# A weight conversion with a scaled exponent, its integer addition on VectorE, and a late reader of a GpSimd maximum

## Chip, cores and metric

One core of one Trainium2 chip runs the whole program. The metric is the device time of one execution in microseconds; the median of 3 runs of the kernel before is 634.65 us (633.98 to 636.14).

## The reference, cut to what matters

Three layers run one after the other on float data (4 batches, 8 heads, 768 steps, head size 48; so 3072 tokens of width 384). The weights of the middle layer (384 x 2048 and 2048 x 384) come in as 64-bit floats.

```python
for t in range(S):                                  # layer 1: linear attention with decay
    cur = einsum('bhd,bhe->bhde', u[None] * kt, vt)
    y[:, :, t] = einsum('bhd,bhde->bhe', rt, state + cur)
    state = wt[..., None] * state + einsum('bhd,bhe->bhde', kt, vt)
h = x @ w_in                                        # layer 2: x is y, 3072 x 384
x = (h * sigmoid(1.702 * h)) @ w_out
logits = x @ phi                                    # layer 3: soft mixture, 8 experts, 32 slots
d = softmax over tokens(logits); slot_input = d.T @ x
slot_out[e] = relu(slot_input[e] @ w1[e]) @ w2[e]
out = softmax over slots(logits) @ slot_out
```

## The kernel before

**Work and stages.** The 3072 tokens are cut into 6 blocks u of 512 (128 steps of each of 4 batches). A block needs 4 attention units (one a batch b; 24 in all, built by unit_nodes), then its share of layer 2 (mm_nodes): for each of 16 slices f of the hidden width, 9 matmuls h (L746), the GELU on ScalarE twice (L750 rounded, L754 full), the remainder on VectorE (L758), 9 matmuls x (L766 to L768). Each 32-bit operand is split into a high and a low part, so 3 matmuls stand for one product. Block 1 is done in two halves of 256 columns. After each block, moe2_nodes updates the running softmax over tokens: transposes, logits (L833), row maxima, exponentials, sums (L892). At the end come the experts (L1100, L1142) and the output (L1182 to L1198).

**Weight conversion.** conv_nodes(f) turns the weights of slice f from 64-bit floats into high and low parts: load raw (L477), ScalarE reads the upper words' magnitude (L482) and scales the lower words down (L483), VectorE clamps (L486), shifts the bits by 3 and masks (L490) and merges the sign (L494), GpSimd or VectorE adds the lower words' bits (L498), ScalarE writes the high part (L501), VectorE the low part (L504). There are two raw buffers and three of the tile cq. In the profiled execution all 16 additions ran on GpSimd.

**Order.** No loop sets the order: every step is a node with a cost, its predecessors, a priority (lower comes first) and buffers taken, and a list scheduler (Plan) simulates the engines and writes each engine's instructions in the order that it finds. Each engine's queue then runs in that order on the chip. Loads are all issued by SyncE (SP), in one queue. Conversion f has priority CONV0 + CONVD * f, attention unit b of block 0 ATT0 + ATTD * b and up to 9 more for its last step, units of block 1 start at 76, layer 2 of block 0 at 42. Loads whose names stand in SOON come first. Steps of VectorE marked port=True and steps of GpSimd exclude each other in the plan, in this form:

```python
if (e == "POOL" or e == "DVE" and s[7]) and port > now + 1e-9:      # L123, in Plan.order
    continue
...
if e == "POOL" or e == "DVE" and s[7]:
    port = free[e]                                                  # L139
```

The GELU remainder (L773) is so marked; the row maximum, softmax and copy steps of moe2_nodes are not.

**The range check.** lim (L570) sums decay factors into chk; inside0 compares them when all units are done, inside1 takes the maximum over partitions on GpSimd (L1023), inside2 reads it on VectorE (L1027), and inside3 loads it into a register at the very end, where a general kernel would run instead if a value were out of range. GpSimd takes two other such maxima: an early one over zeros (L953) and that of the softmax at the end (L1039). At the last attention unit's end GpSimd also has fills and copies (consts3, si0).

Of the kernel before, what the change touches and what calls it, by code (L numbers as in the profile page):

```python
# [8 lines left out]
F32 = mybir.dt.float32  # L9
# [3 lines left out]
AF = mybir.ActivationFunctionType  # L13
ALU = mybir.AluOpType
AX = mybir.AxisListType
PSUM = bass.MemoryType.PSUM

P = 128
NB, NH, NS, DH = 4, 8, 768, 48
DM = NH * DH  # L20
FF = 2048
NF = FF // P
# [7 lines left out]
EPS = 1e-9  # L30
W_TINY, W_HUGE = 2.0 ** -15, 122879.9921875
F_MOST = 2.0 ** 40
RAWB, CQB, NEW = 2, 3, 8

WIDE = (T, T // 2, T, T, T, T)

KTU = (2, 3, 4, 5)
C2E = {"DVE": 1.16, "POOL": 1.95}
RUKE = ({"DVE": 1.12}, {"POOL": 2.1})
QVE = ({"DVE": 0.56}, {"POOL": 1.05})  # L40
PIECES = (192, 192)
# [2 lines left out]
SOON = "w0 r0 c0 n0 u w1 r1 v0 n1 v1 w2 r2 n2 v2 c1 w3 r3 n3 v3"  # L44

FIRST, SECOND, PERIOD, LAG, AHEAD = 42.0, 150.0, 82.0, 4.2, 74.0
CONV0, CONVD, CONVL = 0.0, 6.0, 16.0
ATT0, ATTD = 3.0, 6.0
LAT = {"PE": 0.3, "ACT": 0.25, "DVE": 0.2, "POOL": 0.2, "DMA": 2.2, "X": 0.0}
SAME = {"PE": 0.0, "ACT": 0.2, "DVE": 0.12, "POOL": 0.1, "DMA": 2.2, "X": 0.0}  # L50
FROM = {"PE": 1.9, "ACT": 2.0, "DVE": 1.0, "POOL": 1.0, "DMA": 0.9}
# [3 lines left out]
def act(n):  # L55
    return 0.17 + n / 1200


def dve(n, rate=960):
    return 0.16 + n / rate  # L60
# [294 lines left out]
def rwkv_moe_softmoe_kernel(tc: tile.TileContext, ark, aw, nat, vr, ub, wf, phi, w1, w2, r, k, v, w, ug, out):  # L355
    nc = tc.nc
    pe, ve, ac, gp, sy = nc.tensor, nc.vector, nc.scalar, nc.gpsimd, nc.sync
# [16 lines left out]
    N = plan.add  # L374
    t_ = {}
# [12 lines left out]
    tick = cst.tile([P, 1], F32, name="tick")  # L388
    mfin = cst.tile([P, 1], F32, name="mfin")
    sm = {n: cst.tile([P, NSL], F32, name=n) for n in ("big", "mx", "rz")}  # L390
    chk = sm["rz"][0:ROWS, 0:NU * NB]
    ubt = ap1.tile([P, DM], F32, name="ubt")
    ind = ap1.tile([ROWS, NH, CH], F32, name="ind")
# [3 lines left out]
    m2 = {}  # L397
# [11 lines left out]
    def begin(blk):  # L409
        return FIRST if blk == 0 else SECOND + PERIOD * (blk - 1)  # L410
# [43 lines left out]
    def soon(key, pr):  # L454
        keys = SOON.split()
        return keys.index(key) - 100.0 if key in keys else pr
# [11 lines left out]
    def conv_nodes(f):  # L468
        pr = CONV0 + CONVD * f
        raw, cq, wk = f"raw{f}", f"cq{f}", f"w{f}"  # L470

        def words(t):
            return t_[raw].rearrange("p q n t -> p (q n) t")[:, :, t]

        def load():
            t_[raw] = cp1.tile([P, 2, DM, 2], I32, tag="raw", name=raw, bufs=RAWB)
            sy.dma_start(t_[raw].rearrange("p q n t -> p q (n t)"), wf[2 * f:2 * f + 2].rearrange("q p n -> p q n").bitcast(I32))  # L477

        def c0():
            wt[f] = wp.tile([P, 2, 2 * DM], F32R, tag="w", name=f"w{f}")  # L480
            t_[cq] = cp1.tile([P, 2 * DM], F32, tag="cq", name=cq, bufs=CQB)
            ac.activation(t_[cq], words(1).bitcast(F32), AF.Abs)  # L482
            ac.activation(words(0), words(0).bitcast(U32), AF.Copy, scale=2.0 ** -29)  # L483

        def c1a():
            ve.tensor_scalar(t_[cq], t_[cq], W_TINY, W_HUGE, op0=ALU.max, op1=ALU.min)  # L486

        def c1b():
            a = t_[cq].bitcast(I32)
            ve.tensor_scalar(a, a, 3, 0x3FFFFFF8, op0=ALU.logical_shift_left, op1=ALU.bitwise_and)  # L490

        def c1c():
            a = t_[cq].bitcast(I32)
            ve.scalar_tensor_tensor(a, words(1), -0x40000000, a, op0=ALU.bitwise_and, op1=ALU.bitwise_or)  # L494

        def c2(e):
            a = t_[cq].bitcast(I32)
            onto[e].tensor_tensor(a, a, words(0), op=ALU.add)  # L498

        def c3():  # L500
            ac.activation(wt[f][:, 0], t_[cq], AF.Copy)  # L501

        def c4():
            ve.tensor_tensor(wt[f][:, 1], t_[cq], wt[f][:, 0].bitcast(F32), op=ALU.subtract)  # L504

        n = N("DMA", 2.2, load, pr=soon(f"c{f}", pr - CONVL), take=[("raw", raw)])
        n = N("ACT", 2 * act(2 * DM), c0, [n], pr, take=[("cq", cq), ("w", wk)], use=[raw])
        n = N("DVE", dve(2 * DM, 1920), c1a, [n], pr, use=[cq], port=True)
        n = N("DVE", dve(2 * DM, 1920), c1b, [n], pr, use=[cq], port=True)
        n = N("DVE", dve(2 * DM), c1c, [n], pr, use=[raw, cq], port=True)  # L510
        n = N(C2E, 0, c2, [n], pr, use=[raw, cq], port=True)
        n = N("ACT", act(2 * DM), c3, [n], pr, use=[cq, wk])
        conv[f] = N("DVE", dve(2 * DM), c4, [n], pr, use=[cq, wk], port=True)


    limits, grp_last = [], {}
# [401 lines left out]
    for f in range(NF):  # L918
        conv_nodes(f)
# [23 lines left out]
    tend = begin(NU)  # L943
# [6 lines left out]
    nep = N("X", 0.0, open_ep, att_all, 0)  # L950
# [63 lines left out]


    def inside0():
        t_["cm"] = m2["ep"].tile([P, 2], F32, name="cm")
        ve.memset(t_["cm"], -1.0)
        ve.tensor_scalar(chk, chk, F_MOST, -1.0, op0=ALU.is_le, op1=ALU.mult)
        ve.tensor_reduce(t_["cm"][0:ROWS, 0:1], chk, axis=AX.X, op=ALU.max)  # L1020

    def inside1():
        gp.partition_all_reduce(t_["cm"][:, 1:2], t_["cm"][:, 0:1], P, reduce_op=bass_isa.ReduceOp.max)  # L1023
# [5 lines left out]
    def inside3():  # L1029
        t_["rv"] = nc.values_load(t_["out"][0:1, 0:1], min_val=0, max_val=1, skip_runtime_bounds_check_because="one less a comparison's 0 or 1")  # L1030

    n = nin = N("DVE", 0.35, inside0, limits + [nep], tend - 70)
    n = N("POOL", 0.57, inside1, [n], tend - 29)
    nok = N("DVE", 0.1, inside2, [n], tend - 28)

    G = grp_last
    n = N("DVE", 0.07, f0, [G["mx"]], tend - 59)
    n = N("DVE", 0.16, f1, [n, ncon], tend - 59)
    n = N("POOL", 0.57, lambda: gp.partition_all_reduce(sm["mx"], sm["big"], P, reduce_op=bass_isa.ReduceOp.max), [n], tend - 59)  # L1039
    n = N("DVE", 0.15, f3, [n], tend - 59)  # L1040
    n = N("ACT", 0.12, f4, [n, G["ex"]], tend - 59)
    n = N("DVE", 0.1, lambda: ve.tensor_tensor(sm["mx"], sm["mx"], sel, op=ALU.mult), [n], tend - 59)
# [3 lines left out]
    nsi = N("POOL", 0.68, si0, [nep], tend - 40, take=[("xl", "scrB")])  # L1046
    nsi = nsi0 = N("DVE", 0.17, f7, [n6, nz, nsi], tend - 59, use=["sp", "scrB"])

    finish[0](nsi)


    ctn, cpn = {}, {}
    for u in range(NU):
# [26 lines left out]
        n = N("DVE", 0.66, cs, [cnn[u], nep, cpn.get(u - 2), cpn.get(u - 1)], p0, take=[("xt", "scrA")] if u == 0 else [], use=["scrA"])  # L1080
        n = cpn[u] = N("PE", 0.44, cp, [n], p0, take=[("ps", kp)] + ([] if fin5 else [("a", kp)]), use=["scrA"])
# [7 lines left out]
    for g in range(2):  # L1089
        for hf in range(2):  # L1090
# [27 lines left out]
            n = N("PE", 2.8, e1, [nsi] + [ew[k] for k in keys], p0, take=[("ps", kh)], use=keys + ["scrB"])  # L1118
            own = [ks] if place else ["scrB"]
            n = N("ACT", 0.5, er, [n], p0, take=[(place[0], ks)] if place else [], use=[kh] + own)  # L1120
            n = N("PE", 0.44, et, [n], p0 - 1, take=[("ps", kt)], use=own)
# [4 lines left out]
    c0 = 0  # L1126
    for i, wd in enumerate(PIECES):
# [5 lines left out]
        for g in range(2):  # L1133
# [3 lines left out]
            def e2(p, g=g, ko=ko, wd=wd, at0=at0):  # L1137
                b = t_[ko] if p else bank(ko)
                for n in range(8 * p, 8 * p + 8):
                    a, k, j = at0[n], n // 4, n % 4  # L1140
                    w = t_[f"w2_{a // (4 * DM)}"][:, a % (4 * DM):a % (4 * DM) + wd]
                    pe.matmul(b[32 * j:32 * j + 32, :wd], hv[g]()[:, k, 32 * j:32 * j + 32], w, start=(k == 0), stop=(k == 7))  # L1142
# [8 lines left out]
            n = None  # L1151
            for p in range(4):
                keys = list(dict.fromkeys(f"w2_{a // (4 * DM)}" for a in at0[8 * p:8 * p + 8]))
                at = p0 + 0.5 + p if i and g else p0 - 1 + g + 0.1 * p
                n = N("PE", 0.17 + 0.425 * w_, lambda p=p, e2=e2: e2(p), [n] + hTn[g, p // 2] + [ew[k] for k in keys], at, take=[("ps", ko)] if p == 0 else [], use=keys + [ko])
# [14 lines left out]
        n = N("PE", 0.43 * w_, comp, ns + [ncon3], p0 - 3, take=[("ps", kz)], use=[f"sb{g}{i}" for g in range(2)])  # L1170
        n = N("ACT", 0.06 + 0.1 * w_, skh, [n], p0, take=[("gh", kk)], use=[kz])
        nsk = N("DVE", 0.07 + 0.13 * w_, skl, [n], p0, use=[kk, kz])
        per = min(NB, 512 // wd)
        for u in range(NU):
            kot, oe = f"ot{i}_{u}", []
            for q in range(NB // per):
# [16 lines left out]
                n = N("PE", 0.38 if wd <= P else 0.22, fin, [nsk, ctn[u]], p0 + 3 + u, take=[("ps", kf)], use=[kk])  # L1193
                n = N({"DVE": 0.07 + 0.53 * per * wd / 512, "ACT": 0.06 + 0.42 * per * wd / 512}, 0, oev, [n] + oe, p0, take=[("w", kot)] if q == 0 else [], use=[kf, kot])
# [79 lines left out]
```

## Time and profile before

| what | value |
|---|---|
| median of 3 runs | 634.65 us (633.98 to 636.14) |
| time of the profiled execution | 633.73 us |
| its span, first to last instruction | 631.9 us |
| TensorE busy | 570.4 us (90%) |
| VectorE busy | 431.6 us (68%) |
| ScalarE busy | 274.9 us (44%) |
| GpSimd busy | 90.3 us (14%) |
| mean granted TensorE clock | 0.99 |

PE is TensorE, PEld its weight loads, DVE VectorE, ACT ScalarE, POOL GpSimd, SP SyncE, which issues the loads. Durations come from the one profiled execution; what lies around its span is 1.8 us. A clock of 1.00 is the upper of TensorE's two levels (2.4 GHz), 0.50 the lower (1.2 GHz). Busy TensorE time is modelled and can hold overlaps, so stretches of it are compared by counts of instructions too.

### The profile page before, as it was taken

How to read it: one execution, taken by the hardware profiler on the slowest of the kernel's cores; microseconds unless marked ns; L12 is line 12 of the kernel's file. 1: busy time of each engine (PE TensorE's matmuls, PEld its weight loads, DVE VectorE, ACT ScalarE, POOL GpSimd, SP SyncE). 2: the span in 40 equal slices, each digit the busy share in tenths (PEclk: the TensorE clock that was granted, in tenths of full speed). 3: DMA queues.
4: the chain of work that ended last, by engine and by line, in shares of the span. 5: the costliest groups of instructions: out<-in, count | busy, mean ns of one | idle time of the engine just before them, and what ended most of it. 6: DMA issues, size and time to landing. Idle time of an engine off the chain costs nothing.

```text
span 631.9 us, 12380 instructions
## 1 busy us (share of the span) xinstructions
PE 570.4 (90%) x5092; PEld 462.7 (73%) x5092; DVE 431.6 (68%) x830; ACT 274.9 (44%) x524; POOL 90.3 (14%) x83
## 2 busy tenths in 40 slices
PE   3446899979999999999999999999999969999992
PEld 2445688767889999778877787877788757887362
DVE  9999797899999998787669766787672323112301
ACT  5544566573834443543316432444242333324232
POOL 3121232221111111111012202111120000000000
PEclk9999999999999999999999999999999989999997
DMA  8776434632343333032223232330210294467747
GB/s 294 233 240 209 140 104 158 215 150 76 115 114 114 107 108 113 7 107 74 91 76 101 55 110 77 101 113 28 74 39 1 95 357 147 153 229 249 306 152 219
DMA packets 29475, 86.08 MB, mean 136 GB/s; under 512 B 3040, under 2 KB 12384, under 8 KB 29408
## 3 DMA queue, kind: packets, MB, share of 16 engines
q1 hardware_dynamic: 29408, 85.19, 41.0%
q8 instruction: 42, 0.69, 0.5%
q14 instruction: 25, 0.20, 0.1%
HBM read 80.46 MB, written 4.72 MB: 135 GB/s over the span
## 4 chain that ended last, share of the span: by engine, by line
PE 74%; DVE 14%; issue 4%; DMA 3%; ACT 2%; POOL 1%; SPq 0%; ACTq 0%; DVEq 0%
PE h L746 28%; PE x L766 10%; PE x L767 9%; PE x L768 9%; PE y L652 5%; DMA raw<-in_wf_dram 2%; PE y L654 2%; PE aps L600 2%; PE so L1142 2%; PE eh L1100 2%; PE xps L668 1%; DVE glgh L758 1%; DVE at L574 1%; DVE at L552 1%; PE fo L1182 1%
## 5 line engine op out<-in xcount | busy, mean ns | idle before, releaser
L746 PE MATMUL h<-xth,w 128*128 128x512 f32 (+1 forms) x672 | 205.9, 371 | 3.2 <-ACT w L501 2.0
L750 ACT ACTIVATE ghgh<-h 128x512 fp32r<-128x512 f32 (+1 forms) x112 | 60.0, 537 | 231.7 <-PE h L746 171.0
L746 PEld LDWEIGHTS h<-xth,w 128*128 128x128 f32 x672 | 123.2, 191 | 25.8 <-ACT w L501 2.1
L766 PE MATMUL x<-ghgh,w 128*128 128x512 f32 (+1 forms) x336 | 125.7, 374 | 0.0
L746 PE MATMUL h<-xtl,w 128*128 128x512 f32 (+1 forms) x336 | 122.3, 364 | 0.5 <-DVE xtl L682 0.5
L767 PE MATMUL x<-glgh,w 128*128 128x512 f32 (+1 forms) x336 | 121.7, 362 | 0.6 <-DVE glgh L758 0.4
L768 PE MATMUL x<-ghgh,w 128*128 128x512 f32 (+1 forms) x336 | 121.4, 361 | 0.0
L758 DVE TENSOR_TENSOR glgh<-g,ghgh 128x512 fp32r<-128x512 f32 (+1 forms) x112 | 73.5, 657 | 55.4 <-ACT g L754 54.2
L766 PEld LDWEIGHTS x<-ghgh,w 128*128 128x128 f32 x336 | 63.9, 190 | 11.2 <-issue 0.6
L652 PEld LDWEIGHTS y<-vs,st 128*64 128x64 f32 (+2 forms) x768 | 55.0, 151 | 22.8 <-issue 13.2
L767 PEld LDWEIGHTS x<-glgh,w 128*128 128x128 f32 x336 | 63.9, 190 | 10.5 <-DVE glgh L758 1.9
L746 PEld LDWEIGHTS h<-xtl,w 128*128 128x128 f32 x336 | 64.2, 191 | 9.9 <-DVE xtl L682 1.4
L768 PEld LDWEIGHTS x<-ghgh,w 128*128 128x128 f32 x336 | 63.7, 190 | 9.6
L652 PE MATMUL y<-vs,st 128*64 128x48 f32 (+2 forms) x768 | 61.7, 238 | 9.0 <-DVE ind L551 4.7
L754 ACT ACTIVATE g<-h 128x512 f32<-128x512 f32 (+1 forms) x112 | 59.8, 534 | 4.8 <-DVE glgh L758 3.9
L654 PE MATMUL y<-vs,st 128*48 128x48 f32 (+2 forms) x704 | 50.1, 229 | 0.2 <-ACT st L622 0.2
L659 DVE TENSOR_TENSOR vs<-y,fl 48x384 f32<-48x384 f32 x44 | 24.4, 555 | 37.1 <-PE y L654 36.4
L498 POOL TENSOR_TENSOR cq<-cq,raw 128x768 int32<-128x768 int32 x16 | 32.1, 2008 | 112.2 <-DVE cq L494 52.2
L582 POOL TENSOR_TENSOR nat<-nat 128x384 f32<-128x384 f32 x16 | 16.2, 1012 | 217.4 <-DMA nat<-in_nat_dram 133.7
L654 PEld LDWEIGHTS y<-vs,st 128*48 128x48 f32 (+2 forms) x704 | 44.1, 133 | 0.8 <-ACT st L622 0.6
L600 PE MATMUL aps<-at 48*64 48x64 f32 x768 | 23.6, 239 | 20.5 <-DVE at L574 13.0
L612 DVE TENSOR_TENSOR st<-aps,mask 64x256 f32<-64x256 f32 (+1 forms) x80 | 37.8, 472 | 4.7 <-PE aps L600 3.7
(143 smaller groups left out, 695.8 us busy)
## 6 DMA issues: line engine op xcount, KB each, us to landing
w<-in_w_dram SPq DMA_DIRECT2D x32, 768.0 KB, 5.9
nat<-in_nat_dram SPq DMA_DIRECT2D x24, 576.0 KB, 3.8
raw<-in_wf_dram SPq DMA_DIRECT2D x16, 768.0 KB, 5.3
at<-in_ark_dram SPq DMA_DIRECT2D x24, 512.0 KB, 5.0
at<-in_aw_dram SPq DMA_DIRECT2D x24, 448.0 KB, 4.0
vs<-in_vr_dram SPq DMA_DIRECT2D x48, 96.0 KB, 2.9
out_dram<-ot SPq DMA_DIRECT2D x12, 384.0 KB, 4.0
ubt<-in_ub_dram SPq DMA_DIRECT2D x1, 192.0 KB, 7.5
```

What stands on the lines that cost most here:

```text
L498: onto[e].tensor_tensor(a, a, words(0), op=ALU.add)
L600: pe.matmul(ab[p if four else 0][vl:vh, col:col + CH], t_[a_][lo:hi, 1, 4 * g + h], t_[a_][lo:hi, 0, 4 * g + h], start=True, stop=True)
L612: ve.tensor_tensor(S[0][vl:vh, p, n * g:n * g + n, 0:CH], t_[kap[p if four else 0]][al:ah, 0:n * CH].rearrange("p (h t) -> p h t", h=n), m ...
L652: pe.matmul(yps[vl:vh, cols], S[0][0:k1, p, h, 0:CH], rhs, start=True, stop=True)
L654: pe.matmul(sps[ol:oh, cols], S[0][0:k1, p, h, CH:ROWS], rhs, start=True, stop=True)
L746: pe.matmul(h[:, :wd], a, b, start=(k == 0), stop=(k == len(seq) - 1))
L750: ac.activation(t_[kgh][0], t_[kh][:, :wd], AF.Gelu_apprx_sigmoid)
L754: ac.activation(t_[kg], t_[kh][:, :wd], AF.Gelu_apprx_sigmoid)
L758: ve.tensor_tensor(gl, t_[kg], gh.bitcast(F32), op=ALU.subtract)
L766: pe.matmul(o, whi, gh, start=(f == 0), stop=False)
L767: pe.matmul(o, whi, gl, start=False, stop=False)
L768: pe.matmul(o, wlo, gh, start=False, stop=(f == NF - 1))
```

## The change

In the conversion, ScalarE's read scales the magnitude by 2^-112 and also sums it into a column of wchk; the clamp step is gone; the shift has no mask; the merge takes the sign bit alone; the addition can go to VectorE only and is booked at 0.96 us. inside0 checks the 16 sums too and joins both results. GpSimd's maximum inside1 is booked at 11.5 us for 0.57 and moves to the priority of inside0; its reader inside2 also waits for the last step of si and has a priority behind the end of the last block. The constants of the conversion's and the attention's priorities change.

```diff
--- before.py
+++ after.py
@@ -30,12 +30,13 @@
 EPS = 1e-9
 W_TINY, W_HUGE = 2.0 ** -15, 122879.9921875
 F_MOST = 2.0 ** 40
+W_MOST = 2.0 ** -96
 RAWB, CQB, NEW = 2, 3, 8
 
 WIDE = (T, T // 2, T, T, T, T)
 
 KTU = (2, 3, 4, 5)
-C2E = {"DVE": 1.16, "POOL": 1.95}
+C2E = {"DVE": 0.96}
 RUKE = ({"DVE": 1.12}, {"POOL": 2.1})
 QVE = ({"DVE": 0.56}, {"POOL": 1.05})
 PIECES = (192, 192)
@@ -44,8 +45,8 @@
 SOON = "w0 r0 c0 n0 u w1 r1 v0 n1 v1 w2 r2 n2 v2 c1 w3 r3 n3 v3"
 
 FIRST, SECOND, PERIOD, LAG, AHEAD = 42.0, 150.0, 82.0, 4.2, 74.0
-CONV0, CONVD, CONVL = 0.0, 6.0, 16.0
-ATT0, ATTD = 3.0, 6.0
+CONV0, CONVD, CONVL = 6.0, 4.0, 16.0
+ATT0, ATTD = 3.0, 3.0
 LAT = {"PE": 0.3, "ACT": 0.25, "DVE": 0.2, "POOL": 0.2, "DMA": 2.2, "X": 0.0}
 SAME = {"PE": 0.0, "ACT": 0.2, "DVE": 0.12, "POOL": 0.1, "DMA": 2.2, "X": 0.0}
 FROM = {"PE": 1.9, "ACT": 2.0, "DVE": 1.0, "POOL": 1.0, "DMA": 0.9}
@@ -388,6 +389,7 @@
     tick = cst.tile([P, 1], F32, name="tick")
     mfin = cst.tile([P, 1], F32, name="mfin")
     sm = {n: cst.tile([P, NSL], F32, name=n) for n in ("big", "mx", "rz")}
+    wchk = sm["mx"][:, 0:NF]
     chk = sm["rz"][0:ROWS, 0:NU * NB]
     ubt = ap1.tile([P, DM], F32, name="ubt")
     ind = ap1.tile([ROWS, NH, CH], F32, name="ind")
@@ -479,19 +481,17 @@
         def c0():
             wt[f] = wp.tile([P, 2, 2 * DM], F32R, tag="w", name=f"w{f}")
             t_[cq] = cp1.tile([P, 2 * DM], F32, tag="cq", name=cq, bufs=CQB)
-            ac.activation(t_[cq], words(1).bitcast(F32), AF.Abs)
+
+            ac.activation(t_[cq], words(1).bitcast(F32), AF.Abs, scale=2.0 ** -112, accum_out=wchk[:, f:f + 1])
             ac.activation(words(0), words(0).bitcast(U32), AF.Copy, scale=2.0 ** -29)
-
-        def c1a():
-            ve.tensor_scalar(t_[cq], t_[cq], W_TINY, W_HUGE, op0=ALU.max, op1=ALU.min)
 
         def c1b():
             a = t_[cq].bitcast(I32)
-            ve.tensor_scalar(a, a, 3, 0x3FFFFFF8, op0=ALU.logical_shift_left, op1=ALU.bitwise_and)
+            ve.tensor_scalar(a, a, 3, None, op0=ALU.logical_shift_left)
 
         def c1c():
             a = t_[cq].bitcast(I32)
-            ve.scalar_tensor_tensor(a, words(1), -0x40000000, a, op0=ALU.bitwise_and, op1=ALU.bitwise_or)
+            ve.scalar_tensor_tensor(a, words(1), -0x80000000, a, op0=ALU.bitwise_and, op1=ALU.bitwise_or)
 
         def c2(e):
             a = t_[cq].bitcast(I32)
@@ -504,8 +504,7 @@
             ve.tensor_tensor(wt[f][:, 1], t_[cq], wt[f][:, 0].bitcast(F32), op=ALU.subtract)
 
         n = N("DMA", 2.2, load, pr=soon(f"c{f}", pr - CONVL), take=[("raw", raw)])
-        n = N("ACT", 2 * act(2 * DM), c0, [n], pr, take=[("cq", cq), ("w", wk)], use=[raw])
-        n = N("DVE", dve(2 * DM, 1920), c1a, [n], pr, use=[cq], port=True)
+        n = N("ACT", 2 * act(2 * DM) + 0.2, c0, [n], pr, take=[("cq", cq), ("w", wk)], use=[raw])
         n = N("DVE", dve(2 * DM, 1920), c1b, [n], pr, use=[cq], port=True)
         n = N("DVE", dve(2 * DM), c1c, [n], pr, use=[raw, cq], port=True)
         n = N(C2E, 0, c2, [n], pr, use=[raw, cq], port=True)
@@ -1014,10 +1013,13 @@
 
 
     def inside0():
-        t_["cm"] = m2["ep"].tile([P, 2], F32, name="cm")
+        t_["cm"] = m2["ep"].tile([P, 3], F32, name="cm")
         ve.memset(t_["cm"], -1.0)
         ve.tensor_scalar(chk, chk, F_MOST, -1.0, op0=ALU.is_le, op1=ALU.mult)
         ve.tensor_reduce(t_["cm"][0:ROWS, 0:1], chk, axis=AX.X, op=ALU.max)
+        ve.tensor_scalar(wchk, wchk, W_MOST, -1.0, op0=ALU.is_lt, op1=ALU.mult)
+        ve.tensor_reduce(t_["cm"][:, 2:3], wchk, axis=AX.X, op=ALU.max)
+        ve.tensor_tensor(t_["cm"][:, 0:1], t_["cm"][:, 0:1], t_["cm"][:, 2:3], op=ALU.max)
 
     def inside1():
         gp.partition_all_reduce(t_["cm"][:, 1:2], t_["cm"][:, 0:1], P, reduce_op=bass_isa.ReduceOp.max)
@@ -1029,9 +1031,8 @@
     def inside3():
         t_["rv"] = nc.values_load(t_["out"][0:1, 0:1], min_val=0, max_val=1, skip_runtime_bounds_check_because="one less a comparison's 0 or 1")
 
-    n = nin = N("DVE", 0.35, inside0, limits + [nep], tend - 70)
-    n = N("POOL", 0.57, inside1, [n], tend - 29)
-    nok = N("DVE", 0.1, inside2, [n], tend - 28)
+    n = nin = N("DVE", 0.75, inside0, limits + [nep], tend - 70)
+    nout = N("POOL", 11.5, inside1, [n], tend - 70)
 
     G = grp_last
     n = N("DVE", 0.07, f0, [G["mx"]], tend - 59)
@@ -1046,6 +1047,7 @@
     nsi = N("POOL", 0.68, si0, [nep], tend - 40, take=[("xl", "scrB")])
     nsi = nsi0 = N("DVE", 0.17, f7, [n6, nz, nsi], tend - 59, use=["sp", "scrB"])
 
+    nok = N("DVE", 0.1, inside2, [nout, nsi], tend + 40)
     finish[0](nsi)
 
 
```

## Rows read from the trace of the kernel before

**Rows 1.** Busy tenths of the span in 40 slices of 15.8 us, from the page.

```profile
PE   3446899979999999999999999999999969999992
...
DVE  9999797899999998787669766787672323112301
```

**Rows 2.** Windows by stage: length, busy us (instructions) by engine, granted TensorE clock, DMA share, GB/s.

```profile
0.00:67.00 67.00, 31.27 (x413) 26.48 (x413) 61.88 (x106) 31.43 (x56) 13.77 (x17) 1.00 0.75 242
67.00:160.00 93.00, 87.53 (x661) 70.88 (x662) 80.48 (x117) 57.43 (x97) 22.48 (x12) 1.00 0.42 140
160.00:500.00 340.00, 338.31 (x3176) 281.87 (x3176) 258.37 (x534) 140.66 (x281) 51.80 (x49) 1.00 0.26 79
...
508.60:517.00 8.40, 3.57 (x9) 2.54 (x10) 3.81 (x11) 4.02 (x9) 0.38 (x1) 0.80 0.99 412
```

**Rows 3.** Chain that ended last, in order of time: start us, us, what.

```profile
66.84 9.39 PE h L746 x27
80.31 2.04 PE h L746 x9
...
117.78 7.83 DMA raw<-in_wf_dram
...
502.64 9.52 issue
```

**Rows 4.** Waits, 496 to 530 us: engine, line, for whom, us, times, longest.

```profile
POOL cm L1023 <- issue: 10.4, 1, 10.4
DVE outside L1027 <- POOL cm L1023: 9.9, 1, 9.9
```

**Rows 5.** Lines of the weight conversion: count, shortest/median/longest ns, first and last start.

```profile
L486 DVE TENSOR_SCALAR cq<-cq x16: 551/556/1810, 10.0 to 143.6; 128x768 f32<-128x768 f32 x16
...
L494 DVE SCALAR_TENSOR_TENSOR cq<-raw,cq x16: 937/952/958, 12.2 to 145.9; 128x768 int32<-128x768 int32 x16
...
L498 POOL TENSOR_TENSOR cq<-cq,raw x16: 1817/1914/2727, 14.7 to 147.1; 128x768 int32<-128x768 int32 x16
...
L504 DVE TENSOR_TENSOR w<-cq,w x16: 926/940/960, 18.8 to 151.0; 128x768 fp32r<-128x768 f32 x16
```

**Rows 6.** Chain that ended last, at the tail, from logits to sums.

```profile
580.96 0.47 PE lg L833 x8
...
584.76 0.63 DVE prun L892
```

**Rows 7.** Timeline around the hole: start us, us, engine, line.

```profile
504.18 0.86 PE L833 MATMUL lg<-x2t,phit 128*32 128x128 f32 x24
...
504.78 0.59 ACT L754 ACTIVATE g<-h 128x512 f32<-128x512 f32 x1
...
514.99 1.28 ACT L857 ACT_TABLE_LOAD   x1
```

**Rows 8.** Timeline: a GpSimd addition, and the first and last stretched VectorE instructions.

```profile
14.73 1.82 POOL L498 TENSOR_TENSOR cq<-cq,raw 128x768 int32<-128x768 int32 x1 [10.12 <-DMA vs<-in_vr_dram]
...
15.04 1.93 DVE L590 TENSOR_TENSOR nat<-nat,q 128x384 f32<-128x384 f32 x1
...
147.62 1.58 DVE L758 TENSOR_TENSOR glgh<-g,ghgh 128x256 fp32r<-128x256 f32 x1 [0.45 <-ACT g L754]
```

**Rows 9.** Groups on ScalarE up to 130 us, the accumulator read: busy us, mean ns.

```profile
L570 ACT ACTIVATION_READ_ACCUMULATOR at<-at 112x1 f32 x6 | 1.2, 195 | 0.0
```

**Rows 10.** What ScalarE's first conversion instruction waited for: us, times.

```profile
  DMA raw<-in_wf_dram: 23.0, 10
```

**Rows 11.** Group of the GELU remainder, from the page: busy us, mean ns.

```profile
L758 DVE TENSOR_TENSOR glgh<-g,ghgh 128x512 fp32r<-128x512 f32 (+1 forms) x112 | 73.5, 657 | 55.4 <-ACT g L754 54.2
```

**Rows 12.** GpSimd's maxima (timeline) and its code change (line L582).

```profile
242.20 1.17 POOL L953 PARTITION_ALL_REDUCE pool<-pool  x1 [5.86 <-issue]
...
L582 POOLq MODIFY_POOL_CONFIG  x2: 83/83/83, 243.3 to 243.4; - x2
...
583.22 0.46 POOL L1039 PARTITION_ALL_REDUCE mx<-big  x1 [70.69 <-DVE big L982]
```

## The prediction

> **What bounds the kernel now.** I read the page's slices first, then the windows by stage, the chain that ended last, and the waits and the timeline where the chain left TensorE.
>
> The slices show two regimes [rows 1]: for some ten slices of 15.8 us VectorE is at 7 to 9 tenths and TensorE climbs from 3 to 9; after that TensorE is full, while VectorE empties. The windows give the sizes [rows 2]. Up to 67 us VectorE works 61.9 of 67 us, TensorE 31.3 in short attention matmuls. From 67 to 160 us TensorE loses 93 - 87.5 = 5.5 us and VectorE is busy 80.5 of 93. From 160 to 500 us TensorE loses 1.7 of 340. The dense matmuls begin at 66.84 us in the chain [rows 3]. So the end is set by when TensorE's dense work starts, plus that work, plus every hole in it. Before 160 us the holes are VectorE's doing (weight conversion and attention share it); later a microsecond saved on VectorE is worth nothing.
>
> The one large later hole is in the chain too: 9.52 us of "issue" from 502.64 us [rows 3]. The waits name it [rows 4]: GpSimd's first real maximum (L1023) begins 10.4 us after the operation ahead of it, and its reader L1027, a VectorE instruction that nothing needs before the end, holds VectorE's queue for 9.9 us. Behind it stand the row maximum, the copies out of PSUM and the GELU remainder (L758) without which TensorE cannot go on.
>
> **Term 1: the reader moves.** Between 508.6 and 517.0 us TensorE starts 9 instructions and its mean granted clock is 0.80, a part at the lower of the two levels (1.2 GHz) because it had stood idle [rows 2]. In dense work 9 matmuls take 2.04 us [rows 3]. The hole costs 8.4 - 2.0 = 6.4 us. After the change the reader sits behind the last si (some 80 us later) where the maximum is long done; its one small instruction is below 0.56 us, the price of the 768-column clamp [rows 5], in a queue that waits anyhow.
>
> Not all of 6.4 need come back. The planner now books the maximum at 11.5 us, and a GpSimd step bars VectorE steps marked port=True (L123), which L758 is. In the plan no GELU remainder can start in these 11.5 us, so the softmax steps of block 4, which bear no mark, get ahead of the remainder in VectorE's real queue. The same chain at the tail, from the logits to the accumulated sums, runs from 580.96 to 585.39 us, 4.4 us [rows 6]; here a table load of 1.28 us is added, and the logits begin at 504.18 [rows 7], so it would end near 510. The remainder of the first new group, possible at 505.4 when its GELU ends [rows 7], would wait for that. TensorE meanwhile has two or three h groups of 2.04 us that need no remainder (two h banks), so I put the hole that stays at 1.4 us and take 5.0 us; bounds 2 and 6.4. The three small instructions added to inside0 (16 columns; each below 0.56 us) lie in a stretch where VectorE is busy 3.8 of 8.4 us [rows 2]: nothing, at worst 1.7 us.
>
> **Term 2: the conversion.** Per weight block the clamp goes: 16 x 0.556 = 8.9 us off VectorE [rows 5]. The shift, of the clamp's shape, stays one instruction (0.55), and the sign merge too (0.952). The integer addition leaves GpSimd (1.91 us) for VectorE. The trace has no integer addition there; its nearest rows are the merge with the same strided operand (0.952) and L504 with the same tile (0.940), so 0.95 each: +15.2 us. Bounds from the same rows: 0.55 if it ran like the clamp, 1.9 like GpSimd's; I take the middle, on which both rows with two tensors agree.
>
> What GpSimd's addition did to VectorE comes on top. While it ran, one VectorE instruction at a time was stretched until it ended: L590 at 15.04 took 1.93 us beside the addition of 14.73, L758 at 147.62 took 1.58 [rows 8]; L486 has a median of 0.556 and a longest of 1.81 [rows 5]. I count ten such, these the first and the last, excess over the usual duration 1.38, 1.25, 0.90, 1.09, 1.22, 1.50, 0.75, 0.90, 1.56, 1.16, together 11.7 us. They vanish with the addition. Sum on VectorE: -8.9 + 15.2 - 11.7 = -5.4 us out of a stage where it sets the pace, so I take 5.4 us.
>
> ScalarE: the scale is in the read, which costs as before; the sum output adds an accumulator read, 0.195 us each [rows 9], 16 x 0.195 = 3.1 us. ScalarE is busy 57.4 of 93 us [rows 2], so it is hidden; without that cover 3.1 us is its price. The conversion's chain becomes shorter (no clamp, 0.95 for 1.91 and its queueing), and with it the time that one of two raw buffers is held. That may pay: ScalarE waits 23.0 us for raw weights in ten of the sixteen blocks [rows 10].
>
> **Order.** Block f's conversion had priority 6f and attention unit b the range 3+6b to 12+6b; now 6+4f and 3+3b to 12+3b. Ahead of the last unit of the first block stood conversions 0 to 4, now 0 to 3: about 3.4 us of VectorE (0.55 + 0.95 + 0.95 + 0.94) move behind TensorE's dense start, which I expect at 60 to 62 us for 66.84. That brings nothing by itself, since the work is due later. Behind it all conversions (up to 66) come ahead of the second block's units (from 76). Conversion plus remainder is 3.4 + 0.66 [rows 11] = 4.1 us of VectorE per weight block, and TensorE uses one up in 18 matmuls, 4.08 us [rows 3]: balanced. The raw loads move with the priorities on SP's queue; the loads named in SOON keep their place.
>
> **Sum.** 633.73 - 5.0 - 5.4 = 623.3 us for the profiled execution; the median of the three runs lies 0.9 above it: 624.2.
>
> **A rule against the change.** GpSimd's maximum follows a code change: idle 5.9 us before L953 and 10.4 before L1023, none before L1039, and code is changed back at 243.3 for the next elementwise instruction [rows 4, 12]. The Trainium skill ("GPSIMD Engine Reference", Instruction dispatch) says that the first call of a freshly loaded kernel pays about 6 us that no instruction shows; 5.9 agrees, 10.4 does not. If the new order puts a fill or copy between the two maxima, the page's figure would land on the last one and end the run near 630; the rival below uses the row.
>
> **Rivals.**
> - Only the hole is won; the first stage is bound by latency and loads, not by VectorE's sum. For it: the raw load stands in the chain with 7.83 us [rows 3]. 634.65 - 5.0 = 629.7. Chance 0.17.
> - The first stage gains more: VectorE's idle time up to 160 us (160 - 142.4 = 17.6 us [rows 2]) halves with the shorter chain: 8.8 us more, 615.4. Chance 0.08.
> - The remainder queued behind the softmax keeps the hole: term 1 falls to 0 to 1, about 628.5. Chance 0.05.
> - Other side, starvation between blocks 0 and 1. Dense start at 60, block 0 through by about 128 (65 us of matmuls, 3 of waits). If the second block's units wait for the last conversion at about 120 and two in a row take 25 us, as VectorE's 10 us per unit (61.9 less conversions and stretches, over four) plus their waits make likely, TensorE idles 17 us and restarts slowly: 27 matmuls in 9.39 us at 66.84 where 6.1 is usual [rows 3], 3.3 lost. Against today: 6.8 + 5.5 - 17 - 3.3 = -8.0, with term 1 -3: 637.7. Slower from an idle of about 14 us on. Against it: the units fill VectorE's gaps while ScalarE and loads hold a conversion. Chance 0.08.
> - The late code change: a fill after L1023 makes L1039 pay 10.4 us on the path, 634.6. Against it: consts3 and si0 ran ahead of L1023, whose input is now 0.4 us later still. Chance 0.04.
>
> **Numbers.** The forecast has 0.58. 0.3% of 634.65 is 1.9 us, about what a measurement here tells from no change. Faster: 0.58 + 0.17 + 0.08 + 0.05 = 0.88; same 0.05 (late code change and a mild starvation); slower 0.07. Range: 614 (the larger gain with 1.4 us more of the hole) to 632 (only the hole, at its lower bound of 2 to 3 us).
>
> **What the profile will show.** Right: no VectorE wait at the reader, a hole at block 4's end below 2.5 us, no GpSimd work before 160 us but fills, no stretched VectorE instructions, the addition near 0.95 us, the dense start near 61 us, about the same tail. Wrong if TensorE stands idle for more than 10 us between 110 and 150 us, if L758 waits 5 us behind softmax steps near 495, or if the addition takes over 1.3 us.

## The result and the profile after

The changed kernel takes 616.09 us, the median of 4 runs (615.68 to 617.91), against 635.39 us; the ratio is 0.9698 with a 95% interval of 0.966 to 0.9735. That is faster, inside the range, and 19 us where 10.4 were forecast. Its profiled execution took 615.94 us, with a span of 614.1. Below, a ratio r is also given as (r - 1) x 635.4 us, so that runs beside different runs of the kernel before can be set against each other; the changed kernel stands at -19.2 us. Each such value is uncertain by some 2 us, so a difference between two of them by some 3.

The page's slices of the changed kernel, of 15.4 us each, answer to [rows 1]:

```profile
PE   2465999999999999999999999999999999998992
...
DVE  9989997999998899968768776697572342113201
...
POOL 2000000000130122021102210111210000000000
```

GpSimd shows less than a tenth from the second slice to the tenth, and TensorE is full from the fifth slice on, without the 7 that stood in the ninth. The windows by stage of the changed kernel, with the columns of [rows 2]; the fourth is the stretch in which the hole was:

```profile
0.00:67.00 67.00, 35.18 (x426) 29.44 (x427) 61.91 (x108) 32.68 (x63) 4.01 (x11) 0.72 0.79 249
67.00:160.00 93.00, 92.42 (x780) 76.25 (x778) 84.11 (x138) 67.73 (x129) 2.21 (x3) 1.00 0.44 142
160.00:480.00 320.00, 319.26 (x3004) 266.80 (x3003) 243.84 (x506) 128.93 (x256) 48.29 (x47) 1.00 0.26 82
490.00:500.00 10.00, 9.61 (x80) 7.04 (x78) 5.11 (x17) 7.13 (x14) 0.38 (x1) 1.00 1.01 411
```

Between 67 and 160 us TensorE loses 93 - 92.4 = 0.6 us, where it lost 5.5 [rows 2]. VectorE did not work less up to 160 us but more, 61.9 + 84.1 = 146.0 us for 142.4: its stretches are gone, and 16 additions and other work lie in their place. The two sums don't hold the same work, since the changed kernel is further along by 160 us; over the whole span VectorE's busy time fell from 431.6 to 423.6 us (page). At 490 to 500 us TensorE is idle for 0.4 us. The chain that ended last, in order of time, answers to [rows 3]:

```profile
62.36 7.95 PE h L745 x26
72.35 2.04 PE h L745 x9
...
89.30 6.90 DMA raw<-in_wf_dram
```

The first dense matmul begins at 61.19 us (the chain's row holds the 26 behind it), for 66.84. The 9.52 us of "issue" are gone. When a block's layer 2 is done, ScalarE begins to copy it; these copies are milestones. First the kernel before at the ends of blocks 0, 4 and 5, then the changed kernel (timeline of ScalarE: start us, us):

```profile
161.23 1.57 ACT L804 ACTIVATE x2t<-x 128x512 f32<-128x512 f32 x3
...
500.87 1.97 ACT L804 ACTIVATE x2t<-x 128x512 f32<-128x512 f32 x3 [0.21 <-PE x L768]
...
578.92 1.99 ACT L804 ACTIVATE x2t<-x 128x512 f32<-128x512 f32 x3
```

```profile
140.37 1.28 ACT L803 ACTIVATE x2t<-x 128x512 f32<-128x512 f32 x2
...
487.03 1.97 ACT L803 ACTIVATE x2t<-x 128x512 f32<-128x512 f32 x3 [0.21 <-PE x L767]
...
559.10 1.98 ACT L803 ACTIVATE x2t<-x 128x512 f32<-128x512 f32 x3
```

So the first stage and what follows it up to block 4's end gave 500.87 - 487.03 = 13.8 us. Block 4's end to block 5's end shrank from 78.05 to 72.07 us: 6.0. The tail behind it grew from 52.9 to 55.0 us: 2.0 given back. 13.8 + 6.0 - 2.0 = 17.8 us, the difference of the spans.

The lines of the conversion in the changed kernel, answering to [rows 5] and [rows 9] (count, shortest/median/longest ns, first and last start):

```profile
L485 ACT ACTIVATION_READ_ACCUMULATOR cq<-raw x16: 185/188/206, 7.6 to 123.2; 128x1 f32 x16
...
L490 DVE TENSOR_SCALAR cq<-cq x16: 508/552/561, 10.0 to 125.8; 128x768 int32<-128x768 int32 x16
...
L494 DVE SCALAR_TENSOR_TENSOR cq<-raw,cq x16: 932/952/959, 10.6 to 126.9; 128x768 int32<-128x768 int32 x16
...
L498 DVE CUSTOM_DVE_ANT_0 cq<-raw,cq x16: 931/950/958, 12.6 to 128.4; 128x1536 uint16<-128x1536 uint16 x16
...
L504 DVE TENSOR_TENSOR w<-cq,w x16: 933/958/961, 15.4 to 130.5; 128x768 fp32r<-128x768 f32 x16
```

The addition costs VectorE 0.950 us, as forecast; the compiler made it a custom instruction over 1536 half words. The last low part starts at 130.5 us, for 151.0 [rows 5].

### The profile page after: what moved, and what is told of

It is laid out like the page before. It is cut to its first block, busy times and chain, and to the rows that moved or that the text cites. A ratio compares the mean times of both kernels' runs of the same rounds, so it can differ in the third digit from the quotient of the medians.

```text
span 614.1 us, 12388 instructions
## 1 busy us (share of the span) xinstructions
PE 566.5 (92%) x5092; PEld 460.5 (75%) x5092; DVE 423.6 (69%) x833; ACT 276.8 (45%) x540; POOL 56.8 (9%) x67
## 4 chain that ended last, share of the span: by engine, by line
PE 82%; DVE 7%; DMA 5%; ACT 3%; issue 1%; SPq 0%; ACTq 0%; DVEq 0%
PE h L745 31%; PE x L765 11%; PE x L766 10%; PE x L767 10%; PE y L651 5%; DMA raw<-in_wf_dram 4%; PE aps L599 2%; PE y L653 2%; PE eh L1102 2%; PE so L1144 2%; PE x2t L814 1%; PE xps L667 1%; PE fo L1184 1%; PE pp L884 1%; DVE at L565 1%
## 5 line engine op out<-in xcount | busy, mean ns | idle before, releaser
L757 DVE TENSOR_TENSOR glgh<-g,ghgh 128x512 fp32r<-128x512 f32 (+1 forms) x112 | 71.1, 635 | 59.0 <-ACT g L753 57.8
L745 PEld LDWEIGHTS h<-xtl,w 128*128 128x128 f32 x336 | 64.0, 191 | 10.5 <-DVE xtl L681 2.0
L651 PE MATMUL y<-vs,st 128*64 128x48 f32 (+2 forms) x768 | 60.2, 236 | 2.8 <-DVE st L611 1.8
L599 PEld LDWEIGHTS aps<-at 48*64 48x64 f32 x768 | 20.1, 148 | 23.7 <-DVE at L573 15.8
```

The costliest lines, as they stand in the source:

```text
L599: pe.matmul(ab[p if four else 0][vl:vh, col:col + CH], t_[a_][lo:hi, 1, 4 * g + h], t_[a_][lo:hi, 0, 4 * g + h], start=True, stop=True)
L651: pe.matmul(yps[vl:vh, cols], S[0][0:k1, p, h, 0:CH], rhs, start=True, stop=True)
L745: pe.matmul(h[:, :wd], a, b, start=(k == 0), stop=(k == len(seq) - 1))
L757: ve.tensor_tensor(gl, t_[kg], gh.bitcast(F32), op=ALU.subtract)
```

## The experiments

Each of these kernels ran beside the kernel before on the same chip; the expectations stand as written ahead of each run. "Booked" is the cost that a step has in the plan.

**reader_only.** The kernel before with the moved reader and the maximum booked at 11.5 us.

```diff
-    n = N("POOL", 0.57, inside1, [n], tend - 29)
-    nok = N("DVE", 0.1, inside2, [n], tend - 28)
+    nout = N("POOL", 11.5, inside1, [n], tend - 70)
...
+    nok = N("DVE", 0.1, inside2, [nout, nsi], tend + 40)
     finish[0](nsi)
```

> The kernel before with the moved reader alone (late priority, maximum booked at 11.5 us), conversion and order constants as before. The profile after shows 5.3 us less between the ends of block 4 and block 5, and 1.4 us more in the tail. If the hole is independent of the first stage: 634.6 - 5.3 + 1.4 = 630.7, the tail's loss coming with it. Rival: the tail's loss comes from the first stage's gain, then 629.3.

Measured: 0.9894 (0.9861 to 0.9927), -6.7 us. The copies at the ends of blocks 4 and 5 (timeline of ScalarE) lie 72.07 us apart, as in the changed kernel, for 78.05 before:

```profile
502.10 1.97 ACT L804 ACTIVATE x2t<-x 128x512 f32<-128x512 f32 x3 [0.21 <-PE x L768]
...
574.17 1.97 ACT L804 ACTIVATE x2t<-x 128x512 f32<-128x512 f32 x3
```

The reader's gain stands by itself. Its interval doesn't separate the two expectations, but the tail's 2 us came with it here too (629.2 - 574.2 = 55.0 us), without any gain of the first stage.

**order_only.** The kernel before with the four constants alone.

```diff
-CONV0, CONVD, CONVL = 0.0, 6.0, 16.0
-ATT0, ATTD = 3.0, 6.0
+CONV0, CONVD, CONVL = 6.0, 4.0, 16.0
+ATT0, ATTD = 3.0, 3.0
```

> The kernel before with the four order constants alone. Sum theory (the prediction's): VectorE's total work sets the first stage, order only shifts it, so within 1 us of 634.6. Rival, chain theory: TensorE's holes between 67 and 160 us come from conversions that end late, and putting them ahead of the second block's units fills the holes whatever VectorE's total is: 3 to 6 us faster, 629 to 632.

Measured: 1.0114 (1.0074 to 1.0155), 7.2 us slower. Both theories miss. The window from 67 to 160 us shows the hole that the new order makes while the additions are on GpSimd, 93 - 84.4 = 8.6 us for 5.5:

```profile
67.00:160.00 93.00, 84.38 (x620) 68.89 (x618) 83.02 (x121) 57.91 (x98) 24.95 (x13) 0.96 0.42 136
```

**add_only.** The kernel before with the addition on VectorE alone.

```diff
-C2E = {"DVE": 1.16, "POOL": 1.95}
+C2E = {"DVE": 0.96}
```

> The kernel before with the addition on VectorE alone (clamp, order, reader as before). Sum theory: 16 x 0.95 = 15.2 us more on VectorE, 11.7 us of stretches less, so 3.5 us slower, 638. Chain theory: a link of 1.9 us and its queue becomes one of 0.95 us in VectorE's own queue, the holes get smaller: 0 to 4 us faster, 631 to 635.

Measured: 0.9894 (0.9853 to 0.9935), -6.7 us. The sum theory's sign is wrong. Its window from 67 to 160 us, and the line of the last conversion step:

```profile
67.00:160.00 93.00, 90.81 (x709) 74.42 (x709) 83.94 (x137) 63.98 (x110) 0.11 (x1) 1.00 0.42 135
```

```profile
L504 DVE TENSOR_TENSOR w<-cq,w x16: 935/958/959, 16.5 to 139.3; 128x768 fp32r<-128x768 f32 x16
```

TensorE loses 2.2 us for 5.5, and the last step of the conversions starts 11.7 us earlier, at 139.3, though VectorE is busy 3.5 us longer in that window (83.9 for 80.5). Over the whole span it is busy 430.2 us for 431.6 (page), so the sum theory's 3.5 us more did not come out on the engine either.

**conv_only.** The whole conversion change; order constants and reader as before (the scaling in ScalarE's read, no clamp, the addition on VectorE).

```diff
-CONV0, CONVD, CONVL = 6.0, 4.0, 16.0
-ATT0, ATTD = 3.0, 3.0
+CONV0, CONVD, CONVL = 0.0, 6.0, 16.0
+ATT0, ATTD = 3.0, 6.0
...
-    nout = N("POOL", 11.5, inside1, [n], tend - 70)
+    n = N("POOL", 0.57, inside1, [n], tend - 29)
+    nok = N("DVE", 0.1, inside2, [n], tend - 28)
...
-    nok = N("DVE", 0.1, inside2, [nout, nsi], tend + 40)
```

(against the changed kernel)

> The whole conversion change (scaled read, no clamp, addition on VectorE, check of the sums) with order constants and reader as before. Sum theory: -5.4 us, 629.2. Chain theory: more than VectorE's sum, since clamp and GpSimd link leave the chain: -8 to -11, 624 to 627. If order made the surplus: no more than -5.4.

Measured: 0.9872 (0.9837 to 0.9907), -8.1 us: with the old constants the clamp's end brings 1.4 us beyond the addition's move, less than the intervals can tell.

**reader_back.** The changed kernel with the last two hunks of that diff alone, the early reader.

> The changed kernel with the early reader and the short booking of the maximum as before; conversion and order constants changed. If the reader's gain is independent of the rest (5.7 us measured alone): 616.1 + 5.7 = 621.8. Rival: with the new order the hole overlaps other waits, then under 3 us, below 619.

Measured: 0.9798 (0.9758 to 0.9838), -12.8 us, so the reader is worth 6.4 us on top of the rest: independent within the intervals, as expected.

**order_back.** The changed kernel with the first hunk of that diff alone, the old constants.

> The changed kernel with the four order constants of before. Alone these cost 6.5 us (with the addition on GpSimd). If order and conversion add up, taking the constants back gains: 616.1 - 6.5 = 609.6. If the constants pay only where the addition runs on VectorE: 635.3 - 8.0 - 5.7 = 621.6, so 5.5 us slower than the changed kernel.

Measured: 0.9772 (0.9737 to 0.9806), -14.5 us. The constants are worth 4.7 us here and cost 7.2 alone; they pay only with the changed conversion.

**add_back.** The changed kernel with the addition on GpSimd, booked there.

```diff
-C2E = {"DVE": 0.96}
+C2E = {"POOL": 1.95}
```

> The changed kernel with the addition on GpSimd alone (booked 1.95 us); scaled read, no clamp, order and reader as changed. Sum theory: VectorE loses 15.2 us and gets 11.7 us of stretches: 612.6. Chain theory, with what the single edits measured: 635.3 + 6.5 - 5.7 - 1.3 = 634.8; at least 628.

Measured: 0.9782 (0.975 to 0.9814), -13.9 us: 5.3 slower than the changed kernel. The sum theory falls again by its sign, and the single edits do not add up either: 634.8 was expected from them.

**clamp_back.** The changed kernel with an instruction of the clamp's shape ahead of the shift, booked.

```diff
+        def c1a():
+            ve.tensor_scalar(t_[cq], t_[cq], 0.0, 1.0, op0=ALU.max, op1=ALU.min)
...
+        n = N("DVE", dve(2 * DM, 1920), c1a, [n], pr, use=[cq], port=True)
         n = N("DVE", dve(2 * DM, 1920), c1b, [n], pr, use=[cq], port=True)
```

> The changed kernel with one more VectorE instruction of the clamp's shape per weight block, ahead of the shift (limits 0 and 1, which change no value). Sum theory: 16 x 0.55 = 8.9 us, 625.0. Chain theory, from addition alone against whole conversion (1.3 us): 617.4, at most 620.

Measured: 0.983 (0.9789 to 0.9871), -10.8 us: 8.4 slower than the changed kernel, near the sum theory's 8.9. But the same instruction was worth 1.4 with the old constants. What two edits are worth seemed to depend on the order that the planner found, so the next three experiments keep the order and change the work.

**clamp_same_plan.** The same extra instruction inside the shift's step, unbooked: every queue keeps the changed kernel's order.

```diff
         def c1b():
+            ve.tensor_scalar(t_[cq], t_[cq], 0.0, 1.0, op0=ALU.max, op1=ALU.min)
             a = t_[cq].bitcast(I32)
```

> The changed kernel with the extra instruction of the clamp's shape issued with the shift, not booked in the plan, so that every queue keeps the changed kernel's order. Sum theory: as the booked one, 8.9 us slower than the changed kernel, 625. Plan theory: the booked one lost 8.5 us because the planner found another order; in the old order the 16 instructions lie in VectorE's slack: under 3 us, 617 to 619.

Measured: 0.9763 (0.9729 to 0.9796), -15.1 us: 4.1 slower than the changed kernel, about half of the booked one and half of VectorE's 8.9 us. Between the two theories: a microsecond of VectorE is worth about half of one here, and what clamp_back lost beyond that goes with the planner's order. The intervals of the two runs touch (-17.2 to -13.0 and -13.4 to -8.2); their traces part them, with block 4's end at 492.38 us here and 499.18 in clamp_back, for 487.03 in the changed kernel. TensorE's dense start comes at 63.87 us, for 61.19. The window from 67 to 160 us:

```profile
67.00:160.00 93.00, 90.87 (x724) 74.45 (x723) 87.70 (x146) 67.01 (x125) 0.11 (x1) 0.99 0.43 137
```

**add_back_same_plan.** The changed kernel's order with the addition issued on GpSimd.

```diff
         def c2(e):
             a = t_[cq].bitcast(I32)
-            onto[e].tensor_tensor(a, a, words(0), op=ALU.add)
+            gp.tensor_tensor(a, a, words(0), op=ALU.add)
```

> The changed kernel with the addition issued on GpSimd but booked as VectorE's, so the order of all other instructions stays. Sum theory: 15.2 us off VectorE, stretches back on: 612 to 616. Link theory (the queue of VectorE waits for GpSimd and is stretched by it, and conversions end later): as the booked one, 620 to 623, or worse, since the order doesn't allow for the longer link.

Measured: 0.9763 (0.9724 to 0.9801), -15.1 us: 4.1 slower, with 15.2 us of work off VectorE. Ten VectorE instructions are stretched again, by 12.6 us together; the first and the last, a scan that takes 1.2 us elsewhere and a product of eight columns that takes 0.17 (timeline of VectorE):

```profile
30.89 2.67 DVE L565 TENSOR_TENSOR_SCAN at<-at,ind 112x512 f32<-112x512 f32 x1
...
132.66 0.68 DVE L556 TENSOR_TENSOR fl<-at 112x8 f32<-112x8 f32 x1
```

**add_same_plan.** The kernel before in its own order, with the addition issued on VectorE.

```diff
-            onto[e].tensor_tensor(a, a, words(0), op=ALU.add)
+            ve.tensor_tensor(a, a, words(0), op=ALU.add)
```

> The kernel before with the addition issued on VectorE but booked as before on GpSimd, so the order stays. Sum theory: 3.5 us slower, 638.9. Link theory: about the 6.7 us of the re-planned one, 627 to 630. If the re-planned one gained by its order alone: 635 or more.

Measured: 0.9969 (0.9941 to 0.9996), -2.0 us. None of the theories meets it. The stretches are gone, but the window is the old one, 4.8 us of holes, and the last step of the conversions starts at 151.0 us as before:

```profile
67.00:160.00 93.00, 88.17 (x661) 71.58 (x661) 81.94 (x129) 57.36 (x98) 0.11 (x1) 0.98 0.43 139
```

```profile
L504 DVE TENSOR_TENSOR w<-cq,w x16: 931/942/959, 18.2 to 151.0; 128x768 fp32r<-128x768 f32 x16
```

So of add_only's 6.7 us the engine itself brought 2.0 and the order found for it 4.7; the two intervals, -9.3 to -4.1 and -3.7 to -0.3, do not meet. In the traces of clamp_same_plan, add_back_same_plan and add_same_plan each engine's operations come in the order of the kernel that they start from, but for the 16 added or moved.

**booked_short.** The changed kernel with the maximum booked at 0.57 us.

```diff
-    nout = N("POOL", 11.5, inside1, [n], tend - 70)
+    nout = N("POOL", 0.57, inside1, [n], tend - 70)
```

> The changed kernel with the maximum booked at 0.57 us as before, at its new priority, so that the plan bars no marked VectorE step for 11.5 us. By the prediction's term 1 the booking puts softmax steps ahead of the GELU remainder and leaves 1.4 us: 614.7. Rival: TensorE has enough other work in that time, the booking costs nothing: 615.5 to 617.

Measured: 0.968 (0.9649 to 0.9711), -20.3 us: 1.1 better than the changed kernel by the middle, which the intervals don't settle. The order is as term 1 said. Here the first new GELU remainder starts at 490.82 us, where in the changed kernel it stood until 499.25, behind the row maximum of 491.27 and the softmax (timeline of VectorE):

```profile
490.82 0.68 DVE L757 TENSOR_TENSOR glgh<-g,ghgh 128x512 fp32r<-128x512 f32 x1
```

## Why the prediction was right or wrong

**Term 1, the reader: right, 5.0 forecast, 6.4 to 6.7 measured** (reader_back, reader_only; 6.0 between the copies in the traces). In the changed kernel the reader L1029 runs at 567.43 us, waiting for nothing; the maximum itself still begins 10.5 us after the work ahead of it, and no instruction waits for it. Timeline of ScalarE, VectorE and GpSimd:

```profile
490.94 0.59 ACT L753 ACTIVATE g<-h 128x512 f32<-128x512 f32 x1
...
491.27 0.29 DVE L839 TENSOR_REDUCE mb<-lg 128x1 f32<-128x128 f32 x1 [1.99 <-PE lg L832]
...
499.25 0.68 DVE L757 TENSOR_TENSOR glgh<-g,ghgh 128x512 fp32r<-128x512 f32 x1
...
498.39 0.38 POOL L1025 PARTITION_ALL_REDUCE cm<-cm  x1 [10.50 <-DVE es L879]
563.39 0.46 POOL L1040 PARTITION_ALL_REDUCE mx<-big  x1 [64.62 <-DVE big L981]
...
567.43 0.14 DVE L1029 TENSOR_SCALAR outside<-cm 128x1 int32<-128x1 f32 x1
```

The remainder did fall behind the softmax steps in the queue, as forecast: its GELU ended at 491.53 us, and it stood 7.7 us. That meets one of the prediction's own signs of being wrong (5 us behind softmax steps), but TensorE had other matmuls in that time and lost 0.4 us instead of the 1.4 that I left in place.

**Not forecast: the tail.** The prediction said about the same tail; it grew by 2.0 us. The first group of expert matmuls (48 of L1102, 5.36 us before) took 7.05 us. These are the windows of the 7 us ahead of its start and of 7 and 8 us from it, in the kernel before and in the changed one; from the start on the granted clock is 1.00 and 0.79, so in the changed kernel part of it ran at the lower level (1.2 GHz), after TensorE had been busy 5.08 of the 7 us ahead, where it was 5.40 before:

```profile
579.00:586.00 7.00, 5.40 (x57) 3.51 (x56) 3.06 (x11) 3.59 (x9) 0.46 (x1) 1.00 0.97 339
586.00:593.00 7.00, 6.59 (x60) 2.95 (x60) 2.82 (x11) 1.54 (x4) 0.00 (x0) 1.00 0.46 157
```

```profile
560.00:567.00 7.00, 5.08 (x56) 3.22 (x55) 3.75 (x14) 2.87 (x8) 0.46 (x1) 1.00 0.93 339
567.00:575.00 8.00, 7.91 (x56) 3.07 (x56) 2.18 (x9) 1.67 (x4) 0.00 (x0) 0.79 0.34 111
```

The slow group is not tied to the reader's move. Five of the eight traces with the move have it (6.95 to 7.05 us, for 5.36), and so have reader_back and add_same_plan (7.91 and 6.64) of the six without. The group in the kernel before, the changed kernel, reader_back and clamp_same_plan (chain that ended last):

```profile
586.92 5.36 PE eh L1100 x48
...
567.09 7.05 PE eh L1102 x48
...
575.65 7.91 PE eh L1102 x48
...
572.42 5.36 PE eh L1103 x48
```

Why the clock fell in some and not in others is open.

**Term 2, the conversion, and the order: 5.4 and nothing forecast, 12.8 measured together** (reader_back: -10.3 to -15.4 by its interval). This is where the forecast was short. Two steps failed: "Sum on VectorE: -8.9 + 15.2 - 11.7" as the price of the conversion (8.1 in conv_only), and, of the constants, "That brings nothing by itself" (4.7 by order_back).

TensorE runs the same 3839 matmuls from its first dense one to the copy at block 4's end in all these kernels. So that end is the dense start, plus their busy time, plus TensorE's idle time between. The windows with these two ends, in the kernel before, order_only, conv_only, order_back and the changed kernel:

```profile
66.84:500.87 434.03, 426.87 (x3839) 353.63 (x3840) 339.19 (x651) 198.74 (x379) 74.84 (x64) 1.00 0.29 92
63.08:503.85 440.77, 427.53 (x3839) 355.14 (x3840) 343.19 (x656) 201.05 (x384) 79.28 (x65) 0.99 0.29 94
66.84:492.69 425.85, 424.33 (x3839) 353.11 (x3840) 331.77 (x653) 197.40 (x385) 52.24 (x53) 1.00 0.30 93
65.95:491.38 425.43, 423.99 (x3839) 353.05 (x3840) 331.28 (x653) 197.50 (x385) 52.40 (x53) 1.00 0.30 93
61.19:487.03 425.84, 424.14 (x3839) 352.75 (x3840) 336.15 (x658) 202.04 (x393) 51.06 (x53) 0.99 0.31 96
```

TensorE's idle time there is 434.03 - 426.87 = 7.2 us before. The new conversion with the old constants brings it to 1.5 (conv_only), at the old dense start. With that conversion the constants leave it at 1.7 and move the dense start from 65.95 to 61.19 us; block 4's end follows by 4.35. With the old conversion they move the dense start too, to 63.08, but the idle time grows to 13.2. So in this pair an earlier dense start, with the holes closed, came through to block 4's end nearly whole; that is what "the work is due later" had missed. These are single traces, and they go the way of the measured times.

- The parts were sized right on the engine: the addition takes 0.950 us, the ten stretches vanish (one of 0.8 us at 158.91, beside an attention step on GpSimd, is new), the clamp's 0.55 us are gone. Over the whole span VectorE's busy time fell by 8.0 us all the same, where the sum has 5.4. The Trainium skill ("GPSIMD Engine Reference", Specifications) says that VectorE's instructions in a 2-port mode or with two SBUF inputs contend with GpSimd; the traces agree: stretches of 11.7 and 12.6 us with the additions on GpSimd, none in add_only, add_same_plan or clamp_same_plan.
- What a microsecond there is worth was wrong. Set against VectorE's busy time over the span (pages), the time fits in conv_only (8.4 less, 8.1 us faster), but not in add_only (1.4 less, 6.7 faster) or add_back (5.2 less than the changed kernel, 5.3 slower). In one order the clamp's 8.9 us cost 4.1 (clamp_same_plan), and the addition's +3.5 (by the sum) brought -2.0 in the old order (add_same_plan) and -4.1 in the new (add_back_same_plan, the changed kernel's margin over it). VectorE's sum alone did not set the stage; which of its instructions came first did as well.
- The order was worth as much as the work or more: 4.7 us of add_only's 6.7, about half of clamp_back's 8.4, and the constants' 4.7, which are 7.2 us of loss without the new conversion. Every booked cost gives the planner another order. Shown is that the order carries these microseconds; which rule of the planner does it (GpSimd's additions shut out marked VectorE steps in the plan for their whole 1.95 us, on the chip they stretched ten of some 220 instructions) was only argued.

**Rivals.** "Only the hole is won" falls with reader_back: 12.8 us without the hole's gain. "The first stage gains more" named 615.4 us, nearly the result, but not by its mechanism: VectorE's idle time up to 160 us fell from 17.6 to 14.0 us, not to half. The range reached down to 614 by this rival, so it is in part luck that it holds the result. "The remainder queued behind the softmax" came as a queue, not as a hole. Starvation between blocks 0 and 1 did not come: after 67 us TensorE never waited as long as half a microsecond for the units. order_only comes closer to it: of its TensorE waits between 63 and 162 us, 4.9 us are in attention matmuls (y and aps). The late code change did not come: the fills stayed ahead of the first maximum, and L1040 took 0.46 us as before [rows 12].

**ScalarE's accumulator reads** took 0.188 us each and lay beside other work, as forecast; the dense start came where it was put, 60 to 62 us, but what it was worth was wrong.

## What to carry to other kernels

Where a planner writes the queues, a changed cost changes the order, and the order can be worth more than the cost: measure an edit once with its booking and once in the old order before its price is believed. An engine that is busy nine tenths of a stage need not be the stage's bound; look at which of its results the next engine waits for. An instruction that nobody needs soon, but that waits for another engine, belongs at the end of an in-order queue.

## What was not expected of the hardware

- The 32-bit integer addition on VectorE ran as a custom instruction over 128 x 1536 half words, in 0.950 us, the time of a 768-column two-tensor instruction (0.952).
- The clock column can mislead at the start of a trace: it shows 1.00 for the kernel before over its first 27 dense matmuls, yet these took 9.39 us where 6.1 are usual [rows 3]. Three of them take 1.28 us from 69.30 us on and 0.70 from 73.11 on. The changed kernel's column shows 0.76 over its slow start (26 in 7.95 us from 62.36). First the kernel before, then the changed one (windows):

```profile
66.84:76.23 9.39, 9.39 (x28) 7.34 (x29) 7.45 (x10) 5.49 (x9) 1.85 (x1) 1.00 0.43 147
62.36:70.31 7.95, 7.95 (x27) 6.47 (x28) 7.45 (x12) 5.42 (x10) 0.00 (x0) 0.76 0.54 166
```

- GpSimd's first maximum after other work stood for 10.4 and 10.5 us in both kernels, each time while loads took 0.86 of the DMA engines and more, and 5.9 us when taken early [rows 12], at 0.07 of the DMA engines. The Trainium skill ("GPSIMD Engine Reference", Instruction dispatch) gives about 6 us for the first call of a freshly loaded kernel, which fits the early one alone. Whether the loads make the difference was not tried.
